# The router's rows transposed by DMA as float16 halves, in an attention and mixture-of-experts kernel with float32 scores for the first batch

## The chip, the core and the metric

One core of a Trainium2 chip runs the whole program. The metric is device time in microseconds (us), the median of several executions. Engines: PE (TensorE: matmuls and, as PEld, its weight loads), DVE (VectorE), ACT (ScalarE), POOL (GpSimd) and SP (SyncE, which here only issues DMAs). Each engine runs its own queue of instructions in order and waits for the others by semaphores.

## The reference

Attention with 4 batches, 8 heads, 576 rows of 64, in which each row keeps only its 32 largest scores; then a gated layer; then a mixture of 8 experts, of which each of the 2304 tokens goes to the best two.

```python
x = attn_out.transpose(0, 2, 1, 3).reshape(2304, 512)
x = (sigmoid(x @ w_gate) * (x @ w_val)) @ w_out            # 512 -> 1536 -> 512
noisy = x @ wg + log1p(exp(x @ wn)) * noise                # the router: 512 -> 8, twice
top2, weights = the two largest of noisy, softmax over them
out[token] = sum over its two experts: weight * relu(x @ w1[e]) @ w2[e]   # 512 -> 1024 -> 512
```

## The kernel before

A planner written into the kernel (class `Plan`, lines 49 to 124) orders everything. Each piece of work is an `op` with an engine, a duration, a priority, dependencies, and buffers that it takes (`alloc`) and holds (`use`). `run` simulates the engines and, whenever one is free, emits the ready op of lowest priority number whose buffers are free. The order of emission is the order of each engine's queue; on the chip the times follow from the data. The latency that the plan adds behind an op (`LAT`, line 42, or `lat`) is its guess of when others may use the result. Buffers are counted by tag (`CAPS`, line 177): among them `y=4` and `x2=2` in SBUF and `tp=3` in PSUM.

The work: `attention` (line 310) goes through units of 128 query rows and two heads, with scores on PE, the selection of the 32 largest on DVE with ACT and POOL beside it, transposes and the product with the values on PE. Its POOL product and DVE's last rank use a "y" buffer; its transposes and products use "tp". `moe1` (line 516) takes the rows of a chunk of one or two tiles (128 tokens each, 18 tiles in 12 chunks in all), and does the gated layer with float16 pairs: each float32 operand is a high half and a low half (the rest), and a product is three float16 matmuls. Its priorities put it behind the attention that is due, so PE fills with it.

At the end of `moe1`, each tile goes through these steps, all at a priority that goes before most else:

- `ev` (line 580, ACT): the tile leaves PSUM as float32 rows ("x2", L582), and its high half goes into a "y" buffer (L585).
- `xlo` (line 587, POOL): the low half beside it, from x2 and the high half (L588), at `prio - 1000`.
- `xout` (line 590, SP): the halves, 1024 float16 a row, go to the table `xd` in DRAM, from which the experts gather rows later (L593).
- the router: `rt` (line 607, PE) transposes the four 128x128 blocks of x2 in float32 against an identity into a "tp" buffer (L612); `re` (line 614, ACT) evicts them into a "y" buffer (L616); `rl` (line 618, PE) multiplies them with the router's weights `wr`, 16 columns wide, in float32, as four ops with 0.15 us of planned latency between them (L619). On the trace each of these matmuls is two passes. The logits lie in another "tp" buffer, `q.lg`, taken at the chunk's first transpose.
- `r1` to `r5` (lines 628 to 683): exponential, logarithm and noise, the two best experts, the rank of each token in its expert by small float16 matmuls with a triangle and with ones (L656 to L659), and the entry into the experts' table `tab`.

The experts (`expert`, line 761) read that table, gather rows of xd, and turn them by a DMA transpose of a 128x1024 float16 tile (`turn`, line 789, L790): the same kind and size of transfer as the one of the change. Their matmuls are L804 and L830.

`load_small` and the op behind it (lines 942, 943) fetch `wr` once and scale it on POOL.

Of the kernel before, what the change touches and what calls it, by code (L numbers as in the profile page):

```python
# [11 lines left out]
FT = mybir.dt.float32  # L12
FH = mybir.dt.float16
# [4 lines left out]
OP = mybir.AluOpType  # L18
# [9 lines left out]

SQ, SX, SG, SV, SO, SX2, S1, S2 = 2.0 ** 6, 2.0 ** 6, 2.0 ** 4, 2.0 ** 5, 2.0 ** 6, 2.0 ** 7, 2.0 ** 6, 2.0 ** 6
SPROD = 2.0 * SX * SV  # L30
NEG = -1.0e30


# [94 lines left out]
def attention_moe_kernel(ctx: ExitStack, tc: tile.TileContext, qT, kT, v, w_gate, w_val, w_out,  # L128
# [36 lines left out]

    good = const.tile([128, TILES + 7], FT, name="good")
    wr = const.tile([128, 4, 16], FT, name="wr")
    tok = const.tile([128, N // 128], FT, name="tok")
    for b in range(B):
        G.iota(tok[:, 4 * b:4 * b + 4], pattern=[[128, 4]], base=b * S, channel_multiplier=1,  # L170
# [9 lines left out]
    def layers(fast):  # L180
# [335 lines left out]
        def moe1(ch, prio):  # L516
# [4 lines left out]
            for f in range(12):  # L521
# [35 lines left out]
                d = op("POOL", 0.12 + n / 460, prio - 2000, gl, [c], use=[ht, hg])  # L557
                r.h, r.done = hg, [c, d]
                gs.append(r)
            ch.x2, ch.hx2 = [], []  # L560
            evs = []
            for t in range(nt):
                hm = plan.tile("mm")
# [16 lines left out]
                def ev(r=r, t=t):  # L580
                    x2 = tile_of("x2", [128, DM], FT)
                    A.activation(x2, r.ps, AF.Copy, scale=SX2 / (SPROD * SO))  # L582
                    ch.x2.append(x2)
                    r.xs = tile_of("y", [128, SW], FT).bitcast(FH)[:, :2 * DM]
                    A.activation(r.xs[:, :DM], x2, AF.Copy)  # L585

                def xlo(r=r, t=t):
                    G.tensor_tensor(r.xs[:, DM:], ch.x2[t], r.xs[:, :DM], op=OP.subtract)  # L588

                def xout(r=r, t=t):  # L590
                    for src, q0, q1, tt in ch.rows:
# [1 line left out]
                            nc.sync.dma_start(xd[src:src + q1 - q0, :], r.xs[q0:q1])  # L593
                hxs = plan.tile("y")
                evs.append(op("ACT", 1.1, prio - 2000, ev, last + evs[-1:], alloc=[hx, hxs], use=[hm]))
                a = op("POOL", 1.25, prio - 1000, xlo, [evs[-1]], use=[hx, hxs])
                written.append(op("SP", 1.0, prio - 2000, xout, [a], use=[hxs], lat=3.0))
                ch.hx2.append(hx)

            R = range(nt)  # L600
            hl = plan.tile("tp")
            q = Unit()
            dep = []
            for t in R:
                hp_, hr = plan.tile("tp"), plan.tile("y")

                def rt(t=t):
                    if t == 0:
                        q.lg = tile_of("tp", [128, nt, 32], FT)
                    q.ps = tile_of("tp", [128, 4, 128], FT)  # L610
                    for kb in range(4):
                        P.transpose(q.ps[:, kb, :], ch.x2[t][:, kb * 128:(kb + 1) * 128], ident)  # L612

                def re(t=t):
                    q.xt = tile_of("y", [128, SW], FT)[:, :512].rearrange("p (k f) -> p k f", k=4)
                    A.activation(q.xt, q.ps, AF.Copy)  # L616

                def rl(kb, t=t):
                    return lambda: P.matmul(q.lg[:, t, 0:16], q.xt[:, kb, :], wr[:, kb, :], start=kb == 0, stop=kb == 3)  # L619
                a = op("PE", 0.44, prio - 2000, rt, [evs[t]] + dep, alloc=([hl] if t == 0 else []) + [hp_], use=[ch.hx2[t]],  # L620
                       chain="moe")
                b = op("ACT", 0.5, prio - 2000, re, [a], alloc=[hr], use=[hp_])

                dep = [b]
                for kb in range(4):
                    dep = [op("PE", 0.06, prio - 2000, rl(kb), dep, use=[hr, hl], lat=0.15 if kb < 3 else None, dma=kb < 3)]

            def r1():
                q.sp = small.tile([128, nt, E], FT, name="sp", bufs=2)
                A.activation(q.sp, q.lg[:, :, 8:16], AF.Exp)  # L630
                A.activation(q.sp, q.sp, AF.Ln, bias=one_c)

            def r2():
                q.m8 = small.tile([128, nt, 8], FT, name="m8", bufs=2)
                ix = small.tile([128, nt, 8], U32, name="ix", bufs=2)
                xf = small.tile([128, nt, 2], FT, name="xf", bufs=2)
                V.tensor_tensor(q.sp, q.sp, nst[:, ch.k0:ch.k0 + nt], op=OP.mult)
                V.tensor_tensor(q.sp, q.sp, q.lg[:, :, 0:8], op=OP.add)
                for t in R:
                    V.max(q.m8[:, t], q.sp[:, t])  # L640
                for t in R:
                    V.max_index(ix[:, t], q.m8[:, t], q.sp[:, t])
                V.tensor_copy(xf, ix[:, :, 0:2])
                q.oh = small.tile([128, nt, 2, E], FT, name="oh", bufs=2)
                for t in R:
                    for k in range(2):
                        V.tensor_scalar(q.oh[:, t, k], iota8, xf[:, t, k:k + 1], None, op0=OP.is_equal)
                q.both = small.tile([128, nt, E], FH, name="both", bufs=2)
                V.tensor_tensor(q.both, q.oh[:, :, 0], q.oh[:, :, 1], op=OP.add)
                q.dd = small.tile([128, nt, 2], FT, name="dd", bufs=2)  # L650
                V.tensor_tensor(q.dd[:, :, 0], q.m8[:, :, 1], q.m8[:, :, 0], op=OP.subtract)
# [288 lines left out]
                nc.sync.dma_start(wr[:, :, 8 * a:8 * a + 8], src.rearrange("(k p) e -> p k e", p=128))  # L940
        if fast:
            a = op("SP", 5.0, 26, load_small)
            op("POOL", 0.2, 26, lambda: G.tensor_scalar(wr, wr, 1.0 / SX2, 1.0, op0=OP.mult, op1=OP.mult), [a])

        def init_out(prio):
            q, hz = Unit(), plan.tile("x2")
# [112 lines left out]
```

## Time and profile before

| what | value |
|---|---|
| median of 3 runs | 1325.57 us (1324.25 to 1325.79) |
| the profiled execution | 1323.6 us, span 1321.9 us |
| mean granted TensorE clock | 0.955 |
| PE busy | 1228.2 us, 93% |
| PEld busy | 896.4 us, 68% |
| DVE busy | 869.1 us, 66% |
| ACT busy | 791.6 us, 60% |
| POOL busy | 740.9 us, 56% |
| instructions | 29643 |

The span reaches from the first to the last instruction of the profiled execution; its own time is 1.7 us longer. Busy time is the union of an engine's instructions, without waiting. The page's lines by slices cut the span into 40 equal slices of 33.05 us, and a digit is the share in tenths. The gated layer's last chunk ends at about 900 us; what follows is the experts.

### The profile page before, as it was taken

The page shows a single profiled execution, that of the slowest core. Times are in us where ns is not written, and L with a number is a line of the kernel's source. Part 1 is how long each engine was busy: PE and PEld are TensorE (multiplying, and loading weights), DVE is VectorE, ACT ScalarE, POOL GpSimd, SP SyncE. Part 2 cuts the span into 40 slices and gives each one's busy share as a digit, 9 for nine tenths or more (in the row PEclk, how much of TensorE's full clock was granted, in tenths as well). Part 3 has the DMA queues.
Part 4 walks back from the last instruction along what each step waited for, and adds up shares of the span by engine and source line. Part 5 has one row for each costly group of instructions (what it writes and reads, how often), then busy time and mean ns, then how long its engine had stood idle before and what let it go on. Part 6 is the DMA issues. An engine that isn't in the chain of part 4 may idle for free. (4 is left out here: it accounts for less than half of the span.)

```text
span 1321.9 us, 29643 instructions
## 1 busy us (share of the span) xinstructions
PE 1228.2 (93%) x10669; PEld 896.4 (68%) x10670; DVE 869.1 (66%) x3608; ACT 791.6 (60%) x1788; POOL 740.9 (56%) x1005
## 2 busy tenths in 40 slices
PE   5578799799999999999999999999999999999997
PEld 3347466586776867886777876877666666676674
DVE  6999889998799887888789875455114324233111
ACT  5777678787777877786787774565224324333221
POOL 5989887787476786666676654442222322222221
PEclk9558899899999899999999999999999999999999
DMA  7434331342004310014100003167547576575441
GB/s 222 115 108 122 124 106 27 100 133 112 17 2 101 87 47 10 11 36 121 53 2 2 18 9 97 50 185 204 99 73 194 122 159 171 102 189 132 77 72 22
DMA packets 104463, 119.93 MB, mean 91 GB/s; under 512 B 56561, under 2 KB 65905, under 8 KB 104306
## 3 DMA queue, kind: packets, MB, share of 16 engines
q1 hardware_dynamic: 94194, 97.97, 27.1%
q0 software_dynamic: 10112, 19.97, 8.2%
q8 instruction: 86, 1.41, 0.5%
q14 instruction: 71, 0.58, 0.2%
HBM read 77.22 MB, written 20.63 MB: 74 GB/s over the span
## 5 line engine op out<-in xcount | busy, mean ns | idle before, releaser
L534 PEld LDWEIGHTS <-w 128*128 128x128 f16 x3456 | 276.9, 100 | 38.0 <-issue 12.9
L534 PE MATMUL mm<-xch,w 128*128 128x256 f16 (+1 forms) x2880 | 285.9, 256 | 7.4 <-ACT th L541 3.7
L812 DVE SCALAR_TENSOR_TENSOR g<-mm,g 128x256 f16<-128x256 f32 (+1 forms) x192 | 72.0, 379 | 243.6 <-ACT g L809 233.1
L402 POOL TENSOR_TENSOR y<-sS,sg 128x576 f32<-128x576 f32 x144 | 194.9, 1354 | 9.1
L804 PE MATMUL mm<-xch,w 128*128 128x256 f16 (+1 forms) x2016 | 190.3, 255 | 0.0
L804 PEld LDWEIGHTS <-w 128*128 128x128 f16 x2016 | 170.2, 98 | 23.5
L361 DVE MAX8 cand<-sS 128x8 f32<-128x72 f32 x1152 | 166.8, 217 | 20.6 <-ACT sS L352 20.2
L830 PEld LDWEIGHTS <-g 128*128 128x128 f16 x960 | 92.8, 98 | 106.3 <-DVE g L812 3.4
L573 PE MATMUL mm<-w,g 128*128 128x512 f16 x648 | 158.2, 389 | 1.0 <-POOL w L281 0.7
L424 DVE SCALAR_TENSOR_TENSOR e<-sS,good,e 128x576 f32<-128x576 f32 x144 | 155.5, 1099 | 2.3 <-ACT e L379 1.5
L786 POOL DMA_INDIRECT v<-xd,ids x40 | 47.0, 1175 | 163.5 <-DVE ws L776 155.1
L842 POOL DMA_INDIRECT out<-e,ids x40 | 63.8, 1595 | 131.3 <-ACT e L839 58.6
L809 ACT ACTIVATE g<-mm 128x256 f16<-128x256 f32 (+1 forms) x192 | 65.8, 346 | 112.6 <-PE mm L804 106.6
L551 POOL TENSOR_TENSOR g<-th,g 128x128 f16<-128x128 f32 (+1 forms) x144 | 93.5, 653 | 68.8 <-ACT g L548 65.7
L409 DVE MAX8 good<-y 128x8 f32<-128x584 f32 x144 | 109.9, 763 | 25.8 <-POOL y L402 21.0
L396 ACT ACTIVATE sg<-sS,m 128x576 bf16<-128x576 f32 x144 | 110.7, 770 | 23.5 <-POOL m L387 22.6
L494 PE MATMUL tp<-pt,v 128*64 128x128 f32 (+3 forms) x1600 | 116.9, 285 | 7.0 <-ACT e L379 5.1
L830 PE MATMUL tp<-w,g 128*128 128x512 f16 x504 | 115.6, 379 | 1.7 <-DVE g L812 1.6
L494 PEld LDWEIGHTS tp<-pt,v 128*64 128x64 f32 (+1 forms) x1600 | 85.2, 143 | 41.5 <-issue 23.5
L573 PEld LDWEIGHTS <-g 128*128 128x128 f16 x648 | 63.6, 100 | 67.6 <-issue 9.2
L453 PE MATMUL tp<-ident,e 128*128 128x128 f32 x576 | 91.6, 296 | 17.2 <-DVE e L424 15.7
L379 ACT ACTIVATE e<-sS,m 128x576 f32<-128x576 f32 x144 | 106.5, 768 | 0.2
(160 smaller groups left out, 2073.7 us busy)
## 6 DMA issues: line engine op xcount, KB each, us to landing
st<-w SPq DMA_DIRECT2D x64, 512.0 KB
khl<-st SPq DMA_DIRECT2D x48, 144.0 KB
st<-w_gate SPq DMA_DIRECT2D x12, 512.0 KB
st<-w_val SPq DMA_DIRECT2D x12, 512.0 KB
st<-w_out SPq DMA_DIRECT2D x12, 512.0 KB
out<-x SPq DMA_DIRECT2D x6, 768.0 KB
v<-v_s SPq DMA_DIRECT2D x16, 256.0 KB
xd<-y SPq DMA_DIRECT2D x16, 256.0 KB
```

The costliest lines, as they stand in the source:

```text
L361: V.max(T[t].cand[:, 8 * c:8 * c + 8], T[t].s[:, 72 * c:72 * c + 72])
L379: A.activation(T[t].e, T[t].s, AF.Exp, bias=T[t].m[:, CM:CM + 1], scale=SC[u.b])
L396: A.activation(T[t].sg, T[t].s, AF.Sign, scale=-CUT[0], bias=T[t].m[:, 25:26], accum_out=T[t].m[:, 26:27])
L402: G.tensor_tensor(T[t].y[:, :S], T[t].s, T[t].sg, op=OP.mult)
L409: V.max(good[:, TILES - 1 - u.i - t:TILES + 7 - u.i - t], T[t].y)
L424: return lambda: V.scalar_tensor_tensor(T[t].e, T[t].s, good[:, TILES + 6 - u.i - t:TILES + 7 - u.i - t], T[t].e, op0=OP.is_ge, op1=OP.mul ...
L494: P.matmul(u.po[64 * s:64 * s + 64, :], VB[u.b, kb][1][:k, (2 * u.hp + s) * D:(2 * u.hp + s + 1) * D], rhs, start=kb == 0, stop=kb == NK - 1)
L534: P.matmul(r.ps[:, a, :], wt.t[:, a, c, kb, fo:fo + 128], ch.x[x][:, kb, :], start=i == 0, stop=i == 11)
L551: G.tensor_tensor(r.g[:, 1], r.th, r.g[:, 0], op=OP.subtract)
L573: P.matmul(r.ps, g[:, c, 128 * t:128 * t + 128], WO[f // 4].t[:, d, f % 4, :], start=f == 0 and i == 0, stop=f == 11 and i == 2)
L804: P.matmul(r.ps, W[kb].w[c][:, 0, f * 128:f * 128 + 128], q.x[:, 4 * x + kb, :], start=i == 0, stop=i == 11)
L830: P.matmul(r.ps, gs[f].g[:, c, 128 * t:128 * t + 128], W[4 + f // 2].w[d][:, f % 2, :], start=f == 0 and i == 0, stop=f == 7 and i == 2)
```

## The change

Each tile's halves, which lie as 128 rows of 1024 float16 in a "y" buffer, are transposed by a DMA that SP issues (`xturn`), into a second "y" buffer as eight blocks of 128x128. The router's weights are multiplied by 256 and split into float16 halves, `wrh`. On PE one op of twelve float16 matmuls (high by high, high by low, low by high, for four blocks) takes the place of the four float32 transposes and the four float32 matmuls; the eviction on ACT goes. The scale of the weights is taken out again where the logits are read (`r1`, `r2`). The low half on POOL gets the priority `prio - 2000`. The write of the rows to DRAM comes behind the transpose on SP, and the float32 rows "x2" are no longer held for the router.

```diff
+SR = 2.0 ** 8
...
+    wrh = const.tile([128, 2, 4, 16], FH, name="wrh")
...
-            ch.x2, ch.hx2 = [], []
+            ch.x2 = []
...
-                a = op("POOL", 1.25, prio - 1000, xlo, [evs[-1]], use=[hx, hxs])
-                written.append(op("SP", 1.0, prio - 2000, xout, [a], use=[hxs], lat=3.0))
-                ch.hx2.append(hx)
+                a = op("POOL", 1.25, prio - 2000, xlo, [evs[-1]], use=[hx, hxs])
+                hr = plan.tile("y")
+
+                def xturn(r=r):
+                    r.xt = tile_of("y", [128, SW], FT).bitcast(FH)[:, :2 * DM].rearrange("p (k f) -> p k f", k=8)
+                    nc.sync.dma_start_transpose(r.xt, r.xs)
+                r.turned = op("SP", 1.35, prio - 2000, xturn, [a], alloc=[hr], use=[hxs], lat=3.0)
+                r.hr = hr
+                written.append(op("SP", 1.0, prio - 2000, xout, [r.turned], use=[hxs], lat=3.0))
+                ch.x2.append(r)
...
-                hp_, hr = plan.tile("tp"), plan.tile("y")
-
                 def rt(t=t):
                     if t == 0:
-                        q.lg = tile_of("tp", [128, nt, 32], FT)
-                    q.ps = tile_of("tp", [128, 4, 128], FT)
+                        q.lg = tile_of("tp", [128, nt, 16], FT)
                     for kb in range(4):
-                        P.transpose(q.ps[:, kb, :], ch.x2[t][:, kb * 128:(kb + 1) * 128], ident)
-
-                def re(t=t):
-                    q.xt = tile_of("y", [128, SW], FT)[:, :512].rearrange("p (k f) -> p k f", k=4)
-                    A.activation(q.xt, q.ps, AF.Copy)
-
-                def rl(kb, t=t):
-                    return lambda: P.matmul(q.lg[:, t, 0:16], q.xt[:, kb, :], wr[:, kb, :], start=kb == 0, stop=kb == 3)
-                a = op("PE", 0.44, prio - 2000, rt, [evs[t]] + dep, alloc=([hl] if t == 0 else []) + [hp_], use=[ch.hx2[t]],
-                       chain="moe")
-                b = op("ACT", 0.5, prio - 2000, re, [a], alloc=[hr], use=[hp_])
-
-                dep = [b]
-                for kb in range(4):
-                    dep = [op("PE", 0.06, prio - 2000, rl(kb), dep, use=[hr, hl], lat=0.15 if kb < 3 else None, dma=kb < 3)]
+                        for i, (c, d) in enumerate(((0, 0), (0, 1), (1, 0))):
+                            P.matmul(q.lg[:, t], ch.x2[t].xt[:, 4 * c + kb, :], wrh[:, d, kb, :],
+                                     start=kb == 0 and i == 0, stop=kb == 3 and i == 2)
+                dep = [op("PE", 0.8, prio - 2000, rt, [ch.x2[t].turned] + dep, alloc=[hl] if t == 0 else [],
+                          use=[ch.x2[t].hr] + ([hl] if t else []), chain="moe")]
...
-                A.activation(q.sp, q.lg[:, :, 8:16], AF.Exp)
+                A.activation(q.sp, q.lg[:, :, 8:16], AF.Exp, scale=1.0 / (SR * SX2))
...
-                V.tensor_tensor(q.sp, q.sp, q.lg[:, :, 0:8], op=OP.add)
+                V.scalar_tensor_tensor(q.sp, q.lg[:, :, 0:8], 1.0 / (SR * SX2), q.sp, op0=OP.mult, op1=OP.add)
...
-            op("POOL", 0.2, 26, lambda: G.tensor_scalar(wr, wr, 1.0 / SX2, 1.0, op0=OP.mult, op1=OP.mult), [a])
+
+            def split_router():
+                G.tensor_scalar(wr, wr, SR, 1.0, op0=OP.mult, op1=OP.mult)
+                G.tensor_copy(wrh[:, 0], wr)
+                G.tensor_tensor(wrh[:, 1], wr, wrh[:, 0], op=OP.subtract)
+            op("POOL", 0.6, 26, split_router, [a])
```

## Rows read from the trace of the kernel before

**Rows 1.** The page: busy us and share by engine; DMA share by 40 slices.
```profile
PE 1228.2 (93%) x10669; PEld 896.4 (68%) x10670; DVE 869.1 (66%) x3608; ACT 791.6 (60%) x1788; POOL 740.9 (56%) x1005
...
DMA  7434331342004310014100003167547576575441
```

**Rows 2.** Windows of three stages: us, busy time by engine, clock, DMA share, GB/s.
```profile
0.00:264.40 264.40, 199.24 (x1438) 136.11 (x1440) 233.24 (x861) 190.21 (x412) 217.17 (x279) 0.81 0.39 115
264.40:892.35 627.95, 610.17 (x5966) 473.56 (x5964) 504.61 (x2437) 461.47 (x1094) 412.66 (x646) 0.99 0.20 57
892.35:1322.00 429.65, 418.74 (x3270) 286.69 (x3267) 131.28 (x312) 139.87 (x284) 111.07 (x81) 0.99 0.57 124
```

**Rows 3.** Windows of the router's matmul line L619 alone: PE, then PEld.
```profile
264.40:892.35 627.95, 19.69 (x120) 18.70 (x120) 0.99 0.20 57
0.00:264.40 264.40, 2.57 (x16) 2.25 (x16) 0.81 0.39 115
```

**Rows 4.** Groups by line: busy us, mean ns of one, then idle time before.
```profile
L612 PE MATMUL tp<-ident,x 128*128 128x128 f32 x72 | 11.5, 284 | 0.3 <-ACT x L582 0.3
L619 PE MATMUL tp<-wr,y 128*128 128x16 f32 x144 | 23.4, 245 | 1.4 <-ACT y L616 1.3
L616 ACT ACTIVATE y<-tp 128x512 f32<-128x512 f32 x18 | 10.7, 592 | 1.1 <-PE tp L612 1.1
L534 PEld LDWEIGHTS <-w 128*128 128x128 f16 x3456 | 276.9, 100 | 38.0 <-issue 12.9
```

**Rows 5.** Timeline of PE's weight loads around one tile's router: start, us, what.
```profile
864.15 0.42 PEld L612 LDWEIGHTS tp<-ident,x 128*128 128x128 f32 x4
864.54 2.78 PEld L534 LDWEIGHTS <-w 128*128 128x128 f16 x48
868.14 0.30 PEld L619 LDWEIGHTS tp<-wr,y 128*128 128x128 f32 x2
868.28 0.77 PEld L534 LDWEIGHTS <-w 128*128 128x128 f16 x12
869.00 0.30 PEld L619 LDWEIGHTS tp<-wr,y 128*128 128x128 f32 x2
869.14 0.77 PEld L534 LDWEIGHTS <-w 128*128 128x128 f16 x12
```

**Rows 6.** Timeline of PE at the rank sums of the last tile.
```profile
909.35 0.17 PE L656 MATMUL tp<-both,tri 128*128 128x8 f16 x1
909.38 0.17 PE L659 MATMUL tp<-ohsum,ones 128*128 128x8 f16 x1
909.40 1.46 PE L830 MATMUL tp<-sS,g 128*128 128x512 f16 x6
```

**Rows 7.** Waits over the whole span: total us, times, longest us.
```profile
DVE good L409 <- POOL y L402: 21.0, 22, 3.9
PE tp L453 <- DVE e L424: 15.7, 13, 5.3
PE tp L619 <- ACT y L616: 1.3, 1, 1.3
SPq L593 <- POOL y L588: 198.4, 12, 64.4
```

**Rows 8.** Timeline: low half and row write of the last two tiles.
```profile
863.07 1.16 POOL L588 TENSOR_TENSOR y<-x,y 128x512 f16<-128x512 f32 x1 [1.75 <-ACT y L585]
864.25 0.33 SPq L593 DMA_DIRECT2D xd<-y  x1
895.70 1.16 POOL L588 TENSOR_TENSOR y<-x,y 128x512 f16<-128x512 f32 x1 [1.99 <-ACT y L585]
898.70 0.34 SPq L593 DMA_DIRECT2D xd<-y  x1
```

**Rows 9.** One expert's transpose: its issue, and DMA tenths in 959.9 to 963.4 us.
```profile
959.95 1.23 SPq L790 DMA_TRANSPOSE xch<-v  x1
DMA  0000000000000059999999999999733110000000
```

More of the change, by code (lines that the diff above doesn't have):

```diff
@@ L582, in ev @@
                     A.activation(x2, r.ps, AF.Copy, scale=SX2 / (SPROD * SO))
-                    ch.x2.append(x2)
+                    r.x2 = x2
                     r.xs = tile_of("y", [128, SW], FT).bitcast(FH)[:, :2 * DM]
@@ L587, in xlo @@
                 def xlo(r=r, t=t):
-                    G.tensor_tensor(r.xs[:, DM:], ch.x2[t], r.xs[:, :DM], op=OP.subtract)
+                    G.tensor_tensor(r.xs[:, DM:], r.x2, r.xs[:, :DM], op=OP.subtract)
                 def xout(r=r, t=t):
```

## The prediction

> **What bounds the kernel now.** I read the page's busy shares first. PE is busy 93% of the span [rows 1], more than any other engine, but the share is a mean over stages, so I cut the span in three with the windows view [rows 2]. Up to 264 us (weights prepared, attention of the first batch and part of the second) PE is idle 65 us, and DVE and POOL are the fuller engines. From 264 to 892 us PE is busy 610.17 of 627.95 us: 17.8 us idle, against 123 us on DVE, the next. After 892 us, in the experts, it is idle 10.9 us. So a microsecond taken off PE's queue between 264 and 892 us is a microsecond off the end, as long as nothing makes PE wait in its place; the same microsecond on ACT, POOL or SP is worth nothing.
>
> How much of the router lies there? The windows view of the router's matmul line counts 120 instructions of 144 in the middle stretch, 15 of the 18 token tiles, and 16 (two tiles) before it [rows 3]; the last tile lies in the experts' stretch, which PE bounds too. So 16 tiles count and two do not.
>
> **The change part by part.** *Removed from PE.* The duration in a PE row isn't its price, because matmuls overlap: the transposes are busy 11.5 us and the float32 matmuls 23.4 us [rows 4], yet both lie partly under their neighbours. I take the pitch instead, from the start of one group of weight loads to the next group's start, in a stretch where PE had no gap [rows 5]. Four transposes: 864.15 to 864.54, 0.39 us. A router matmul is two float32 passes: 868.14 to 868.28 and 869.00 to 869.14, 0.14 us for each of four, 0.56 us. Together 0.95 us a tile, 15.2 us over 16 tiles.
>
> *Added to PE.* Twelve float16 matmuls a tile: a 128x128 weight load from the transposed rows, 16 columns moving. No row has 16 columns. The nearest is the 128x8 float16 matmul of the rank sums, each with a fresh 128x128 load: starts at 909.35, 909.38 and, of what follows, 909.40, so 0.03 and 0.02 us apart [rows 6]. The bound above is the 128x128 float16 matmul, twelve from 868.28 to 869.00, 0.06 us each [rows 5]. I take 0.03, the pitch nearest in columns: 0.36 us a tile, 5.8 us over 16. Ends kept for the range: 0.02 gives 3.8 us, 0.06 gives 11.5 us. **Net on PE: 15.2 - 5.8 = 9.4 us**, between 3.7 and 11.4 us.
>
> The price of the load is where the Trainium skill speaks against the change. "TensorE: Matmul & The Clock Gate", section on LDWEIGHTS, prices a weight load by its 128 columns at some 107 ns, whatever moves afterwards; by that, twelve would cost an estimated 1.28 us a tile and the sum would be a loss. The pitches of 0.02 to 0.06 us disagree; the case is rival 4.
>
> *ACT.* The eviction of the transposed rows goes, 18 of 592 ns [rows 4], 10.7 us. ACT is idle 166 us in the middle stretch [rows 2], so I count nothing for it; all that PE felt of it is 1.3 us of waiting at the router's matmuls [rows 7]. That goes.
>
> *POOL.* The low half, 1.16 us [rows 8], moves ahead of attention's work by its new priority, and is now on the router's path. Eighteen of them put attention's POOL work back by 1.2 us at a time, under a POOL idle for 215 us of the stretch [rows 2]: nothing there, and up to 1 us before 264 us. The two operations added to the preparation of the weights are smaller than this one and run once, on POOL: 0, or at most 1 us if the first stage feels them. The scale moved into the router's exponential and sum adds no instruction: nothing.
>
> *SP.* Each tile gains a transpose, whose issue is 1.23 us on the queue [rows 9], 22 us in all. What is behind it starts that much later: the tile's own rows to DRAM, then loads; in a chunk of two tiles the second transpose also stands behind the first tile's row write. SP waited 198 us in 12 places for exactly the POOL operation that would release the transpose [rows 7], so at most tiles its queue is empty and nobody behind is late: nothing.
>
> *The path of one tile.* Before: POOL's low half starts at 863.07, PE's transposes at 864.15, and the last pair of router matmuls comes after 869.14, since the planner lays a dozen other matmuls between the pairs [rows 5, 8]. After: the low half ends at 864.23 and SP can issue at 864.25, as it did the row write. The transpose of the same size that SP issued at 959.95 moves bytes in slices 15 to 28 of a window of 3.5 us from 959.9, thus from 961.1 to some 962.5 [rows 9]: 2.6 us from issue. So the tile stands transposed at 866.9, and the twelve matmuls follow in one block: no later than now. The planner puts them 1.35 + 3.0 us behind SP's start, which leaves a margin of 1.75 us. I charge no wait but one: at the last tile SP reached the row write only at 898.70, though the low half ended at 896.86 [rows 8], and the DMA engines are seven tenths busy in that slice [rows 1]. I put 1.3 us on it, which cancels the wait that goes.
>
> *Buffers.* The logits' "tp" buffer, one of three in PSUM, is now taken at the matmuls (866.9 above) and not at the first transpose (864.15), and the second "tp" not at all. Of "y", four buffers, a two-tile chunk can now hold all (two halves, two transposed), where attention wants them too. I set both at zero, the gain and the loss; each is a rival.
>
> **Sum.** 15.2 off, 5.8 on, waits even, two early tiles nothing: 9.4 us. The profiled execution took 1323.6 us (span 1321.9), 2.0 under the median of 1325.57; off the median that gives **1316.2 us**.
>
> **Rivals.**
> 1. *PSUM frees attention.* PE's waits in the middle stretch, such as the 15.7 us in all for DVE's masked scores [rows 7], shrink when "tp" buffers come back some 3 us earlier in each of 12 chunks. A third of the 17.8 us idle would give 6 us more: 1310.2. Against: the wait that is listed has another engine for its releaser, not a buffer. Chance 0.12.
> 2. *The gain is eaten.* The plan is laid out anew, "y" is short, and attention's chain over DVE, which is busy 505 of 628 us, sets the pace in more places; PE's saved time turns into idle time, all or all but 3 us of it: 1322.6 to 1325.6. For: DVE already waits 21.0 us for POOL's product in "y" [rows 7]. Against: PE has other matmuls to fill with. Chance 0.15.
> 3. *PE waits for the transpose: slower.* PE's queue is in order, and what stands behind a late block stands still. It decides from a landing 4.35 + 0.59 = 4.9 us after SP's start, where the wait eats that tile's gain. A mean wait of 0.8 us over 16 tiles is 12.8 us against 9.4: 1329.0. For: the DMA engines are three to four tenths busy in the slices around 428 us and six to seven at the last two tiles, and the transpose queues behind that. Against: in the slices of most other tiles they are at 0 or 1 [rows 1]. Chance 0.13.
>  The Trainium skill's "VectorE: DVE Perf Modes", section on the three transpose paths, has the DMA crossbar at 1309 ns for one 128x128 block against 390 ns on TensorE and advises TensorE; eight blocks one by one would be an estimated 10.5 us. The row above moves eight in 1.4 us, so I give that no chance of its own.
> 4. *Loads bound the twelve.* If each took the 100 ns that a weight load's own row has [rows 4], a tile would cost 1.2 against 0.95 us, 4.0 us more over 16: 1329.6. The pitches speak against it: chance 0.02. This is the case that the LDWEIGHTS rule would make.
>
> **The numbers.** A measurement of this kernel tells about 0.2%, 2.65 us, from no change. The forecast has 0.58; its own range, from the two ends of the price, is 1314.2 to 1321.9. Faster: 0.58, rival 1's 0.12 and 0.04 of rival 2. Same: 0.10 of rival 2 and 0.03 of rival 3. Slower: 0.10 of rival 3, 0.02 of rival 4, 0.01 of rival 2. The range, 1310.0 to 1324.5, reaches down to rival 1 and up over most of rival 2; left out are rivals 3 and 4 and the edges of the others.
>
> **What would show it.** Right: the router's float16 matmuls start 0.02 to 0.04 us apart; the stretch that ends with the last tile's router comes to its end 8 to 11 us earlier, with PE's idle time near 18 us; the twelve start under 4.4 us after SP's issue; the experts' stretch keeps its length. Wrong: PE waiting for the transposes by over 10 us in all (rival 3); a pitch near 0.1 us (rival 4); idle under 13 us (rival 1); 6 us or more of new waits for DVE, POOL or ACT (rival 2).

## The result, and the profile after

The change made the kernel slower: 1337.01 us (median of 4 runs, 1334.43 to 1339.00) against 1325.21 us (4 runs, 1324.25 to 1325.79), a ratio of 1.0089 (95%: 1.0068 to 1.0109). The forecast was 1316.2 us, the range ended at 1324.5. Two executions in a slow state, one of e13 below (6740 us) and one of the kernel before (2047 us), are left out of all medians and ratios here. A ratio is an estimate from all the other executions, and can differ by some 0.2% from the quotient of two medians. The profiled execution took 1334.43 us, span 1332.7 us: 10.8 us longer than the span before.

The page of the kernel after, busy time of PE and the DMA slices, for [rows 1]:

```profile
PE 1218.6 (91%) x10669; PEld 881.9 (66%) x10670; DVE 865.1 (65%) x3608; ACT 782.3 (59%) x1770; POOL 740.9 (56%) x1007
...
DMA  7334341352104501042200123275647567576441
```

PE does lose work, 1228.2 to 1218.6 us: 9.6 us. The time went up all the same, so PE idles some 20 us more. The clock is not the reason: the mean granted TensorE clock was 0.974 in this execution, 0.955 before. Where PE idles, the windows view tells, cut finer than [rows 2] (columns: window, its length, then busy time of PE, PEld, DVE, ACT, POOL with instructions, granted clock, DMA share, GB/s). The kernel before:

```profile
264.40:845.00 580.60, 565.36 (x5437) 438.28 (x5435) 479.97 (x2349) 434.34 (x1032) 391.65 (x616) 0.99 0.18 52
845.00:892.00 47.00, 44.47 (x530) 35.08 (x530) 24.29 (x89) 27.12 (x63) 20.78 (x30) 0.96 0.47 130
892.00:960.00 68.00, 67.91 (x534) 47.76 (x533) 25.39 (x78) 25.13 (x51) 18.59 (x17) 1.00 0.66 151
960.00:1308.00 348.00, 346.26 (x2706) 236.59 (x2705) 105.67 (x232) 113.50 (x230) 91.17 (x64) 1.00 0.57 123
```

The kernel after:

```profile
264.40:845.00 580.60, 560.02 (x5549) 432.48 (x5548) 483.86 (x2396) 431.91 (x1035) 389.15 (x620) 1.00 0.22 58
845.00:892.00 47.00, 40.46 (x461) 30.94 (x459) 20.46 (x54) 23.53 (x52) 21.02 (x27) 0.96 0.49 135
892.00:960.00 68.00, 57.98 (x453) 39.72 (x453) 22.36 (x71) 22.75 (x45) 18.41 (x15) 0.95 0.67 149
960.00:1308.00 348.00, 345.77 (x2664) 235.72 (x2663) 105.98 (x233) 112.29 (x228) 89.19 (x63) 1.00 0.57 123
```

The length less PE's busy time is PE's idle time: 15.2, 2.5, 0.1 and 1.7 us before, 20.6, 6.5, 10.0 and 2.2 us after. So three places lose: the middle 5.4 us, the stretch of the last two tiles' gated layer 4.0 us, and the 68 us in which the last tile is handed to the experts 9.9 us. The later experts lose nothing to speak of (0.5 us). Of the 4.0 us some 2 are no more than what one such trace differs from the next: the controls e4, e7 and e8 below, which do the work of before in nearly its order, idle 4.2 to 4.4 us in 845 to 892 us.

**The price was right.** PE's weight loads around one tile's router, of the kernel after (start, us, what), for [rows 5]:

```profile
863.92 0.41 PEld L619 LDWEIGHTS <-y 128*128 128x128 f16 x12
864.26 1.79 PEld L536 LDWEIGHTS <-w 128*128 128x128 f16 x32
```

The twelve loads hold the queue for 0.34 us (863.92 to 864.26), where the transposes and the four float32 matmuls took 0.95.

**The handover.** The last tile's way in the timeline of the kernel after, for [rows 6, 8]:

```profile
893.94 1.16 POOL L590 TENSOR_TENSOR y<-x,y 128x512 f16<-128x512 f32 x1 [0.81 <-ACT y L587]
895.46 5.04 SPq L786 DMA_TRANSPOSE xch<-v  x2
900.60 0.53 SPq L711 DMA_DIRECT2D st<-w  x1
901.18 1.23 SPq L603 DMA_TRANSPOSE y<-y  x1
905.58 0.46 PE L619 MATMUL tp<-wrh,y 128*128 128x16 f16 x12 [0.77 <-DMA y<-y]
912.40 0.18 PE L652 MATMUL tp<-both,tri 128*128 128x8 f16 x1
915.75 0.17 DVE L673 CAST sl<-slf 128x2 int32<-128x2 f32 x1
```

The low half ends at 895.10. The plan has put two transposes of an expert's rows and a weight load ahead of the tile's transpose on SP, so this is issued at 901.18, 6.1 us later, and its matmuls start at 905.58. Before, PE did the tile without SP; from the same view of the kernel before:

```profile
895.05 0.62 PE L612 MATMUL tp<-ident,x 128*128 128x128 f32 x4
...
902.69 0.29 PE L619 MATMUL tp<-wr,y 128*128 128x16 f32 x2
```

So the low half stands 1.8 us earlier than before (893.94 against 895.70), and the last of the router's matmuls ends 3.1 us later (906.04 against 902.98). What follows is worse. POOL's timeline, after:

```profile
912.39 2.66 POOL L838 DMA_INDIRECT out<-e,ids  x1 [17.29 <-ACT e L835]
921.31 1.59 POOL L838 DMA_INDIRECT out<-e,ids  x1 [6.26 <-DMA out<-e,ids]
923.21 0.99 POOL L677 DMA_INDIRECT tab<-wk,sl  x1 [0.31 <-issue]
924.21 0.34 POOL L865 IOTA y<- 1x104 f32 x1
926.69 1.01 POOL L677 DMA_INDIRECT tab<-wk,sl  x1 [2.15 <-DMA tab<-wk,sl]
```

and before:

```profile
911.62 1.00 POOL L681 DMA_INDIRECT tab<-wk,sl  x1 [14.76 <-DVE sl L677]
912.92 1.70 POOL L842 DMA_INDIRECT out<-e,ids  x1 [0.30 <-issue]
914.05 0.63 POOL L869 IOTA y<- 1x104 f32 x1
916.12 1.02 POOL L681 DMA_INDIRECT tab<-wk,sl  x1 [1.44 <-DMA tab<-wk,sl]
```

The tile's two entries into the experts' table are L681 before, L677 after; L842 and L838 are the additions of expert 0's results to the output. Before, the first entry heads the queue. After, both stand behind two additions, and the second addition waits 6.3 us for the first one's transfer. The slots are known at 915.9 (L673), yet the entries go at 923.21 and 926.69, 11.6 and 10.6 us later than before. Behind them stand an iota, DVE's limits of the blocks and an eviction, so PE stops:

```profile
926.46 7.07 PE L800 MATMUL mm<-xch,khl 128*128 128x256 f16 x48 [7.21 <-DVE g L808]
```

### The profile page after: what moved, and what is told of

The parts are those of the page before. It is cut to its first block, busy times and chain, and to the rows that moved or that the text cites. A ratio compares the mean times of both kernels' runs of the same rounds, so it can differ in the third digit from the quotient of the medians.

```text
span 1332.7 us, 29623 instructions
## 1 busy us (share of the span) xinstructions
PE 1218.6 (91%) x10669; PEld 881.9 (66%) x10670; DVE 865.1 (65%) x3608; ACT 782.3 (59%) x1770; POOL 740.9 (56%) x1007
## 5 line engine op out<-in xcount | busy, mean ns | idle before, releaser
L404 POOL TENSOR_TENSOR y<-sS,sg 128x576 f32<-128x576 f32 x144 | 191.2, 1328 | 9.1
L426 DVE SCALAR_TENSOR_TENSOR e<-sS,good,e 128x576 f32<-128x576 f32 x144 | 149.0, 1057 | 3.5 <-ACT e L381 2.4
L838 POOL DMA_INDIRECT out<-e,ids x40 | 65.0, 1625 | 148.1 <-ACT e L835 80.4
L553 POOL TENSOR_TENSOR g<-th,g 128x128 f16<-128x128 f32 (+1 forms) x144 | 96.5, 674 | 62.7 <-ACT g L550 60.9
L354 ACT ACTIVATE sS<-ps 128x576 f32<-128x576 f32 x144 | 92.6, 643 | 31.0 <-PE ps L338 15.3
```

The source lines that it names most:

```text
L404: G.tensor_tensor(T[t].y[:, :S], T[t].s, T[t].sg, op=OP.mult)
L426: return lambda: V.scalar_tensor_tensor(T[t].e, T[t].s, good[:, TILES + 6 - u.i - t:TILES + 7 - u.i - t], T[t].e, op0=OP.is_ge, op1=OP.mul ...
L553: G.tensor_tensor(r.g[:, 1], r.th, r.g[:, 0], op=OP.subtract)
```

## The experiments

Each expectation (set off as a quotation) names its theories by letters. Those that carry the verdict: A2, the entries behind the additions; F, the row write behind the transpose on SP; I, PE's time is the kernel's time; K, the plan's new order of the queues; L, the transposes themselves (traffic, SP, waits). "Before" was run beside each; ratios are to it, with a 95% interval.

**e1: the iota out of the way.** The limits are made once at the start.

```diff
+    G.iota(thr_c, pattern=[[0, E], [BLK, NB]], base=CAP, ...)
...
-                G.iota(thr, pattern=[[0, E], [BLK, NB]], base=CAP, ...)
```

> The changed kernel, with the one row of block limits that the counting of tokens needs (an iota on POOL) made once at the start instead of in POOL's queue behind the experts' additions; the plan is the same. Theory A (the loss lies at the handover from the gated layer to the experts, 7.2 us of it because DVE waits 7.8 us for that iota, which now stands behind a scatter-add in POOL's queue): DVE's wait of 7.8 us and PE's idle 7.2 us at 919 to 926 us are gone; the next thing late is the transposed rows of expert 0's third block, 2 to 3 us, so 4 to 7 us faster than the changed kernel: 1330 to 1333 us. Theory B (the wait is harmless, since the experts wait for the last tile's rows anyway): PE is idle as long, a few us later; 1336 to 1338 us.

Measured: 1337.05 us, 1.0095 (1.0064 to 1.0126). The stall of 7.2 us is gone and nothing is won. In 892 to 960 us PE is busy 62.56 us; it stops later instead, for the third block of expert 0, whose rows depend on the entries:

```profile
932.62 1.04 PE L828 MATMUL tp<-sS,g 128*128 128x512 f16 x4 [2.55 <-DVE g L810]
...
943.41 2.86 PE L802 MATMUL mm<-xch,khl 128*128 128x128 f16 x31 [2.89 <-DMA xch<-v]
```

So theory A fell: the wait that the profile names last was not the cause. Whether the late entries were, which both waits trace back to, is for e5.

**e2 and e3: which tiles.** e2 keeps the new path but for the last two chunks, which go through PE as before; e3 does the reverse.

```diff
+            old = nchunk[0] > 10      # e3: nchunk[0] <= 10
...
```

> The changed kernel, with the last two chunks (one tile each) routed as before: float32 transposes and matmuls on PE, eviction on ACT, the row write straight behind the low half; the other ten chunks keep the DMA transposes. Theory A (loss at the handover: the last two tiles' longer path over POOL, SP and the DMA queue reorders POOL, SP and DVE there): the handover is again as in the kernel before and the other 16 tiles keep 0.5 us each of PE time less some 5 us of new idle time: 1321 to 1326 us, 11 to 16 us faster than the changed kernel. Theory C (the new plan loses all along, by the shortage of y buffers in the middle): 1334 to 1338 us.

> The converse: the kernel before, with only the last two chunks' tiles by the DMA transpose and float16 halves. Theory A (handover): nearly the whole loss comes with these two tiles, 8 to 14 us over the kernel before: 1333 to 1339 us. Theory C (loss in the middle, by y buffers): 1324 to 1327 us.

Measured: e2 1327.29 us, 1.0018 (1.0006 to 1.0031); e3 1327.69 us, 1.0034 (1.0023 to 1.0046). Neither is what theory A asked. e2 gives back some 9 us (1.0089 to 1.0018) and ends just above A's range; e3 loses only 3 to 5 us with these two tiles alone on the new path, where A asked for 8 to 14, and lies nearer to C. So the last two tiles cost 3 to 9 us, by what order the rest of the plan has, and the ten other chunks on the new path win nothing either. e2's windows, the middle and the handover:

```profile
264.40:845.00 580.60, 561.72 (x5558) 433.94 (x5557) 484.34 (x2396) 432.67 (x1035) 390.12 (x620) 0.99 0.21 58
...
892.00:960.00 68.00, 63.05 (x477) 42.51 (x475) 22.19 (x73) 22.07 (x45) 17.19 (x14) 0.97 0.61 134
```

18.9 us idle in the middle against 15.2 before, and 5.0 us at the handover, although its last tiles go the old way.

**e4: e1's edit in the kernel before**, as a control.

```diff
+    G.iota(thr_c, ...)
```

> Control: the kernel before, with the row of limits made at the start. There DVE waits only 1.0 us for the iota. Theory A: no more than that to win, 1324 to 1326 us. If it gains 3 us or more, what the first experiment gains is no repair of the change but a gain that both kernels could have.

Measured: 1324.08 us, 0.9996 (0.9985 to 1.0008): no difference.

**e5: the entries ahead of the additions.** e1's edit, and expert 0's additions depend on the last entry.

```diff
-add, [a] + added[-1:], use=[he, ht]
+add, [a] + added[-1:] + (entered[-1:] if e == 0 else []), use=[he, ht]
```

> The first experiment's kernel (changed kernel, limits made at the start), in which expert 0's scatter-additions on POOL wait, in the plan too, for the last entry into the experts' table. Theory A2 (at the handover the last tile's entries stand in POOL's in-order queue behind two scatter-additions, the second of which waits 6 us for the first to land; so the table of expert 0's third block is read at 929 to 930 us, not 920): the entries are issued right after the slots are known, near 917 us instead of 923 to 924, the table read comes 5 to 8 us earlier, PE's idle time between 850 and 960 us falls from 15 to under 9 us; 1329 to 1333 us. Theory D (the last tile's transpose, which stands on SP behind the experts' transposes and loads, sets it): at most 2 us gained, 1335 to 1338 us.

Measured: 1326.85 us, 1.0030 (1.0019 to 1.0040). Against e1, whose edit it contains, that is 0.65% or 8.6 us given back by one dependency, more than A2's range had asked. POOL's timeline, and the windows from 264 us:

```profile
916.86 1.00 POOL L679 DMA_INDIRECT tab<-wk,sl  x1 [18.41 <-DVE sl L675]
920.09 0.97 POOL L679 DMA_INDIRECT tab<-wk,sl  x1 [2.24 <-DMA tab<-wk,sl]
921.37 1.60 POOL L840 DMA_INDIRECT out<-e,ids  x1 [0.30 <-issue]
```

```profile
264.40:845.00 580.60, 559.56 (x5546) 432.21 (x5544) 481.11 (x2396) 432.16 (x1034) 389.47 (x620) 1.00 0.21 58
845.00:892.00 47.00, 37.80 (x436) 27.49 (x434) 19.45 (x53) 21.81 (x50) 21.56 (x27) 0.93 0.45 133
892.00:960.00 68.00, 67.67 (x542) 47.56 (x540) 26.48 (x79) 25.81 (x52) 18.27 (x16) 1.00 0.67 152
```

The handover is full again (0.3 us idle). A2 stands, and D falls: the tile's transpose is no earlier here (901.59 us) and its matmuls start at 906.40, so that the entries still go 5.2 and 4.0 us later than before, and PE does not wait for that. What cost the time was the additions ahead of the entries, not the tile's delay by itself. Still idle are 21.0 us in the middle and 9.2 us before 892 us, 12.5 us more than in the kernel before and 10 to 11 more than in e4, e7 and e8.

**e7: e5's edits in the kernel before.**

```diff
+    G.iota(thr_c, ...)
...
+add, [a] + added[-1:] + (entered[-1:] if e == 0 else []), use=[he, ht]
```

> Control: the kernel before with the same two edits as the fifth experiment (limits at the start, expert 0's additions behind the last entry). There the entries were issued ahead of the additions but for one. Theory A2: 1322 to 1326 us, no difference to the kernel before. If it gains 3 us or more, the fifth experiment's gain is not the repair of what the change did.

Measured: 1326.11 us, 1.0008 (0.9990 to 1.0026). The kernel before had its entries in front already, but for the last, which stood behind one addition.

**e6 and e15: the "y" buffers.** The transposed rows go into an "x2" buffer (e6; e15 adds e5's edits).

```diff
-                hr = plan.tile("y")
+                hr = plan.tile("x2")
...
```

> The changed kernel with the transposed rows in an x2 buffer (free after the low half) instead of a fourth y buffer. Theory C (in the middle, y is short: SP's transposes wait for attention's rank to free a y, and attention waits for y in turn, which made PE's idle time from 264 us to attention's end 20.6 us, not 15.2): SP's waits for DVE's rank vanish, idle time there falls back to 14 to 17 us; 1331 to 1334 us. If y is not it: idle stays at 20 us or more, 1335 to 1339 us.

> The fifth experiment's kernel (limits at the start, expert 0's additions behind the last entry) with the transposed rows in x2 buffers as in the sixth. Theory C as a second, small cause (y): 2 us under the fifth, 1323 to 1326 us. If nothing else than y were wrong: 1316 to 1320 us. If y is no cause: 1326 to 1329 us.

Measured: e6 1334.90 us, 1.0076 (1.0055 to 1.0098); e15 1330.19 us, 1.0051 (1.0033 to 1.0069), no better than e5. The waits on SP's queue do show the shortage of "y": the first row is the kernel after, the second e6.

```profile
SPq L603 <- DVE good L411: 241.0, 7, 68.3
```

```profile
SPq L603 <- POOL y L590: 296.8, 10, 76.0
```

In e6 the wait for DVE, which reads the "y" buffer last, is gone, SP waits for the low half in its place, and the time is nearly the same: a wait of 241 us on a queue that nobody needs earlier is worth next to nothing. In 264 to 845 us PE does idle less, 18.0 us in e6 against 20.6 and 17.3 in e15 against 21.0 in e5, but in e6 it idles 70.4 us before 264 us, not 65.4: "y" moves the idle time more than it takes it away.

**e8: the low half's priority alone, in the kernel before.**

```diff
-                a = op("POOL", 1.25, prio - 1000, xlo, [evs[-1]], use=[hx, hxs])
+                a = op("POOL", 1.25, prio - 2000, xlo, [evs[-1]], use=[hx, hxs])
```

> The kernel before with one part of the change alone: the low half's priority on POOL ahead of attention's. It takes no work away; it shifts the plan. Theory A2 (the loss has its place at the handover and its cause in the transposes' longer path): 1323 to 1327 us. Theory E (any shift of the plan costs as much, the order of before was a lucky one): 1330 us or more.

Measured: 1323.51 us, 0.9994 (0.9978 to 1.0010). So the low half's priority costs nothing by itself, and not every new layout of the plan costs time.

**e9, e10 and e12: the row write and the planned times.** e12 puts the row write ahead of the transpose; e9 adds e5's edits; e10 gives the plan nearer times as well.

```diff
-r.turned = op("SP", 1.35, prio - 2000, xturn, [a], alloc=[hr], use=[hxs], lat=3.0)
-written.append(op("SP", 1.0, prio - 2000, xout, [r.turned], use=[hxs], lat=3.0))
+written.append(op("SP", 1.0, prio - 2000, xout, [a], use=[hxs], lat=3.0))
+r.turned = op("SP", 1.35, prio - 2000, xturn, [written[-1]], alloc=[hr], use=[hxs], lat=3.0)
...
-op("PE", 0.8, prio - 2000, rt, [ch.x2[t].turned] + dep,    # e10 alone, with lat=2.0 at the transpose
+op("PE", 0.36, prio - 2000, rt, [ch.x2[t].turned] + dep,
```

> The changed kernel with the row write ahead of the transpose and nothing else. Theory F as the second place of the loss beside A2: 2 to 6 us faster than the changed kernel, 1331 to 1335 us, with the entries still behind the additions. Theory F as the whole loss: 1322 to 1326 us. If it does nothing: 1336 to 1338 us.

> The fifth experiment's kernel, with the tile's row write on SP ahead of its transpose, as it stood straight behind the low half in the kernel before. Theory F (the second place of the loss: at the last tile but one the row write, now behind the transpose, is caught behind the experts' first gather, which reads the same table in DRAM; the next gather waits 4.2 us for the write's landing in POOL's queue, and the gated layer's low halves, ACT and PE behind it, so that attention's end to the last tile's eviction takes 46 to 50 us, not 41): the gather's wait for the row write goes, that stretch takes 41 to 45 us, and the kernel takes 1319 to 1324 us, level with the kernel before or faster. If F is wrong: 1326 to 1329 us, as the fifth experiment.

> The ninth experiment's kernel, in which the plan reckons with what the trace of the changed kernel shows: 0.36 us for the twelve matmuls instead of 0.8, and 3.35 us from SP's start of the transpose to its landing instead of 4.35 (measured 3.1 in the middle). Theory G (part of the lengthening is the plan's own, which sets the router's steps later than the data come): another 1 to 3 us, 1317 to 1322 us. If the plan's figures don't matter, the same as the ninth within 2 us; PE could also meet transposes that are late, and then L619's waits for the DMA would exceed 5 us in all.

Measured: e12 1336.29 us, 1.0084 (1.0064 to 1.0103); e9 1325.89 us, 1.0013 (0.9996 to 1.0030); e10 1329.65 us, 1.0041 (1.0024 to 1.0057). In the time, F is worth nothing that can be told apart: e9's interval overlaps that of e5. In the trace its place is real. e5's row write at the last tile but one, POOL's second gather behind it, and PE's longest wait of the stretch:

```profile
864.01 0.33 SPq L597 DMA_DIRECT2D xd<-y  x1
866.39 0.97 POOL L784 DMA_INDIRECT v<-xd,ids  x1 [4.25 <-DMA xd<-y]
879.99 5.28 PE L577 MATMUL mm<-w,g 128*128 128x512 f16 x12 [4.99 <-DVE th L548]
```

In e9 no gather waits for the write, and PE idles 3.8 us of 845 to 892 us instead of 9.2, as little as the controls. But it idles 3.0 us at the handover (0.3 in e5) and 72.1 us before 264 us (67.6 in e5): the repair of one place is paid back in others. Nearer durations (e10) made it no better than e9: the order that comes out is another, not a better one.

**e11: e2 with e5's edits.**

```diff
+            old = nchunk[0] > 10
...
+add, [a] + added[-1:] + (entered[-1:] if e == 0 else []), use=[he, ht]
```

> The second experiment's kernel (last two chunks routed on PE) with the limits at the start and expert 0's additions behind the last entry. Theory A2 (with the old path in the last two tiles the handover is sound but for its rank sums): 1321 to 1326 us. Theory H (the ten chunks by DMA save 8 to 9 us of PE time and keep it if the handover doesn't take it back): 1316 to 1320 us.

Measured: 1327.86 us, 1.0025 (1.0013 to 1.0037). That is above both ranges. Both ways of mending the end reach the same 1327 us, and adding them up gains nothing more, so H falls: the PE time that the ten chunks save is lost outside the handover.

**e13 and e14: the price of the router in the kernel before.** e13 does one block of four (transpose, eviction and matmul), e14 each matmul three times, in the order of before. PE's other work stays: its instructions fall by the 162 left out, and rise by the 288 put in.

```diff
-                    return lambda: P.matmul(q.lg[:, t, 0:16], q.xt[:, kb, :], wr[:, kb, :], ...)
+                    return lambda: kb or P.matmul(q.lg[:, t, 0:16], q.xt[:, 0, :], wr[:, 0, :], ...)  # e13
+                        for i in range(3): P.matmul(...)  # e14
```

> The kernel before, its plan unchanged to the last op, but of each tile's router only the first of four blocks is transposed, evicted and multiplied (three quarters of the logits' sum are left out, so tokens go to other experts). It takes 3 x 0.10 + 3 x 0.14 = 0.72 us a tile off PE, 11.5 us over 16 tiles, more than the change takes off, with neither DMA transposes nor another order. Theory I (PE's time is the kernel's time in the middle, and the change loses its saving by its transposes and its order): 1313 to 1317 us. Theory J (attention's chain over ACT, DVE and POOL takes up what PE saves): 1319 to 1324 us, with 5 us or more of new idle time on PE.

> The kernel before, its plan unchanged, each of the router's four matmuls made three times (the logits are three times too large, so tokens go to other experts): 8 x 0.14 = 1.12 us a tile more on PE, 18 us over 16 tiles. Theory I: 1338 to 1344 us. Theory J: 1329 to 1335 us, PE's idle time falls.

Measured: e13 1314.09 us (median of five), 0.9937 (0.9918 to 0.9955); e14 1355.84 us, 1.0263 (1.0233 to 1.0293). In e13 three quarters of 0.95 us in 16 tiles are 11.4 us, and 8 to 9 us came off, within I's range. e14 lies above I's range, for the most part because I had the price too low: three matmuls of a block take 0.59 us of weight loads in its trace (862.92 to 863.51), so each of the two that were added takes 0.22 us and not 0.14, or 28.8 us over 16 tiles. The medians differ by 32.5 us, and the spans of the two profiled executions by 28.0, with PE busy 29.6 us longer (1257.8). Theory I stands and J falls: where the order stays, what PE has less or more to do shows in the time, for the most part or more.

**e16: the plan of e5 without transposes.** SP's op is there for the planner and does nothing; PE reads a constant tile.

```diff
-                    nc.sync.dma_start_transpose(r.xt, r.xs)
+                    return
...
-                            P.matmul(q.lg[:, t], ch.x2[t].xt[:, 4 * c + kb, :], ...
+                            P.matmul(q.lg[:, t], tri, ...
```

> The fifth experiment's kernel with its plan unchanged to the last op, but the DMA transposes are left out, and the twelve float16 matmuls read a constant 128x128 tile (the router's logits are then not those of the tokens; noise sends the tokens to the experts). Theory K (the order that the new plan gives costs the new idle time, whatever the transposes do): idle time from 264 us to attention's end stays at 19 to 22 us, 1323 to 1328 us. Theory L (the transposes themselves cost it: late landings, SP's issue, the DMA queue, y buffers held): that idle time falls to 15 to 17 us and the handover's to under 6 us, 1314 to 1319 us.

Measured: 1326.90 us, 1.0027 (1.0013 to 1.0042), as e5. Its windows:

```profile
264.40:845.00 580.60, 560.01 (x5559) 432.97 (x5557) 478.33 (x2397) 432.31 (x1034) 389.62 (x621) 1.00 0.17 52
845.00:892.00 47.00, 37.78 (x418) 27.66 (x417) 19.28 (x53) 21.55 (x48) 20.39 (x25) 0.89 0.41 129
```

The idle time is that of e5 (20.6 and 9.2 us), with none of the router's transposes on any queue. L falls: neither these transfers nor waiting for them makes the rest of the loss. What is left is the order of the queues, as K says, the row write's place among it, which is as late here as in e5. The last tile's matmuls, too, start at 905.98 us, though they wait for no transfer: it is the plan that sets them so late. The waits of PE from 264 to 850 us show its form; the kernel after, then before:

```profile
PE mm L536 <- ACT th L543: 5.8, 7, 1.5
PE ps L346 <- ACT sS L354: 5.3, 6, 1.4
PE tp L473 <- POOL px L445: 4.9, 4, 1.7
```

```profile
PE ps L344 <- ACT sS L352: 4.8, 8, 1.8
PE mm L534 <- ACT th L541: 3.7, 4, 1.7
```

Four places in which PE waits for attention's product on POOL are new, and the gated layer's waits for ACT are 3 more.

**e17: the chunks between by DMA.** The first two and the last two chunks go through PE, with e5's edits.

```diff
+            old = nchunk[0] > 10 or nchunk[0] <= 2
```

> The eleventh experiment's kernel with the first two chunks routed on PE as well, so that only eight chunks (14 tiles) of the middle go by the DMA transpose; their float16 matmuls save some 8 us of PE. If the early stage's 2 to 5 us of new idle time come from the first two tiles: idle time before 264 us back at 65 us, 1321 to 1325 us. Theory K: it is as much an accident of the order as the rest, 1324 to 1329 us.

Measured: 1329.32 us, 1.0039 (1.0023 to 1.0056). PE idles 27.0 us in 264.4 to 845 us, more than with all chunks by DMA, and 67.7 us before 264 us, not 65: one more order, and a worse one.

**e18: the new work in the plan of before.** The ops of before stay in the plan, the transposes' and the eviction's empty; each group of three float16 matmuls takes the place of a float32 one, and the DMA transpose is put in ahead of the row write at nearly no planned time.

```diff
+                r.turned = op("SP", 0.3, prio - 2000, xturn, [a], alloc=[r.hr], use=[hxs], lat=0.0)
...
-                dep = [b]
+                dep = [b, xr.turned]
```

> The change's instructions in a plan as near as possible to that of the kernel before: the plan still reckons with the float32 transposes, the eviction and four matmuls of before (0.44, 0.5 and 4 x 0.06 us) and lays the router's four steps out as then, three float16 matmuls in each; the transpose stands on SP behind the low half and ahead of the row write, without planned latency; the eviction's place on ACT is empty. Theory K (the order of the changed plan cost the saving and more): idle time from 264 us to attention's end near 15 us plus the waits for transposes that come after the planned place, 3 to 8 us in all; the handover as before; 1316 to 1322 us, faster than the kernel before. If the order of before was no better, or the waits for the transposes grow past 10 us: 1325 to 1332 us.

Measured: 1346.35 us, 1.0163 (1.0149 to 1.0177): a miss, the slowest of all that do the same work. Here PE does wait for the transposes; a row of its waits, and the last tile's timeline:

```profile
PE tp L625 <- DMA y<-y: 14.5, 6, 7.9
```

```profile
908.41 1.16 POOL L590 TENSOR_TENSOR y<-x,y 128x512 f16<-128x512 f32 x1 [1.12 <-ACT y L587]
912.04 1.23 SPq L798 DMA_TRANSPOSE xch<-v  x1
...
913.95 1.23 SPq L603 DMA_TRANSPOSE y<-y  x1
...
918.46 0.25 PE L625 MATMUL tp<-wrh,y 128*128 128x16 f16 x3 [7.87 <-DMA y<-y]
```

PE meets the matmuls where the old path had them ready; the new one reaches them through SP, so they come late, 7.9 us at the last tile. The old order does not fit the new path: the transposes cost nothing in the kernel after because the plan sets the matmuls later; that this is what shifts all else I argue from it, and no run shows it by itself. The waits for transposes are 14.5 of the 22 us that e18 loses; what makes the rest stays open. The test that would show the order alone, e18 with its transposes left out as in e16, was not run.

No version that does the whole work is faster than the kernel before; of those with the new path, only e9 has an interval that reaches down to it.

## Why the prediction was wrong

- *The price on PE: right.* 9.4 us forecast; 1228.2 to 1218.6 is 9.6. The pitch of the twelve is 0.34 us over twelve, 0.028 each, where 0.03 was taken; 0.95 less 0.34 is 9.8 us over 16 tiles. That 9.4 and 9.6 lie so close is luck, though, for busy times differ by some us where the work on PE is the same: 1222.8 to 1230.9 in the kernel before, e4, e7 and e8.
- *"So a microsecond taken off PE's queue … is a microsecond off the end": right only for an order that stays.* e13 and e14 show it within before's order. The condition set behind it (as long as nothing makes PE wait in its place) is what did not hold. The change alters durations, latencies, buffers and dependencies in the plan, and the plan lays out all queues anew.
- *"The path of one tile … no later than now": the step that failed.* I worked it out at the last tile but one, where SP was free, and put the waits as even. At the last tile SP's queue held two transposes and a load ahead, so the transpose was issued 6.1 us after its release. I charged 1.3 us for this queue and took PE's wait for its only price. PE's wait was small (0.8 us); the price was the tile's place in the queues, which the plan sets (e16 has it as late without the transfer). Its logits came 3.1 us later than before, the plan let expert 0's additions go ahead of its table entries, and those went 10.6 and 11.6 us late. e5 shows that the additions' place, not the delay, cost 8.6 us. The experts' stretch begins with a wait; the sign "the experts' stretch keeps its length" did not come.
- *"SP … nothing", "POOL … nothing": wrong in kind.* A queue that is empty on average is full where the work changes hands. That the entries of the last tile share POOL's queue with additions I had not looked at.
- *Waits even in the middle: wrong by some 5 us,* and by 2 to 7 us at the last two tiles. e16 shows this loss with none of the router's transposes issued. At the last two tiles the row write behind the transpose has a part in it (e5 and e9), a term that the prediction put at nothing. Rival 2 said it (all or nearly all of the gain eaten by a new plan), but ended at 1325.6; e5, with the handover mended, is about there. Which of the plan's new entries makes the order worse stays open: the low half's priority (e8, in the kernel before), "y" (e15), the row write (e9) and the durations (e10) were each tried; the first costs nothing, and none of the others gives the gain back.
- *The landing at 2.6 us: a little short.* The slices of [rows 9] that are not 0 run on to 962.8 us, 2.8 us from the issue; the transposes of the change landed after 2.8 to 4.9 us, median 3.1. The median is within the margin of 1.75 us, the longest is not; PE hardly felt either.
- *Rival 1* fell, for PE's idle time grew. *Rival 3* fell for the kernel after: PE's matmuls wait 0.8 us in all for the transposes, their weight loads 1.6. e18 shows its mechanism at work, 14.5 us, where the order does not allow for the transfer. *Rival 4* fell by the pitch. The Trainium skill's "TensorE: Matmul & The Clock Gate", section on LDWEIGHTS, prices a load at some 107 ns by its 128 columns. In the trace of the kernel after a load of the router lasts 96 ns (median), near the page's figure, but the next begins 28 ns later: the duration is not what one more load costs.

## What to carry to other kernels

In a kernel whose queues are laid out by a planner, price a change in two steps: what the bounding engine has less to do, and then the new order, which can eat more than the gain. Look at the last item that the next stage waits for, and follow it through every in-order queue that it crosses, for a delay of 3 us there can let other work in ahead of it and become 11. Mending one such place need not show in the time (e9), where the new order pays for it elsewhere. A long wait in the profile is not yet a cost (SP's 241 us), and taking away the last wait of a chain (e1) only shows the next one.

## What the runs showed of the hardware

The transfer's median lies below the 4.35 us that the plan reckons with, its longest above. The transposes of 128x1024 float16, from issue to landing (min, median, max), in the kernel after:

```profile
DMA to landing us min/median/max: 2.8/3.1/4.9
```

The Trainium skill's "VectorE: DVE Perf Modes", section on the three transpose paths, has 1309 ns for one 128x128 block on the DMA crossbar; by that, eight would be an estimated 10.5 us one by one. The trace disagrees with that sum: eight in one transfer took 3.1 us.

Float32 matmuls of 16 columns cost more back to back than spread out: in e14 three on the same block take 0.59 us from the first weight load to the next group's, where [rows 5] have 0.14 us for one among float16 ones. PE's busy time bears it out: the 144 that e14 adds (two for each of 4 in 18 tiles) make it 29.6 us longer, 0.21 us each, with some 0.05 either way by which busy times differ. Why they cost more, no run here shows.
